# Another order for the 1290 steps of one kernel, other engines for a third of its small steps, and 19 fillers on TensorE where there were 48

## The chip, the cores and the metric

The kernel runs on one core of a Trainium2 chip. The metric is device time in microseconds (us). TensorE (PE in the profile) multiplies, VectorE (DVE), ScalarE (ACT) and GpSimd (POOL) do the elementwise work, and SyncE (SP) starts the transfers. Each engine carries out its own instructions strictly in the order in which the program gives them; engines wait for each other only where data or a buffer is concerned.

## The reference

Three stages follow each other, in float32:

```
attention (mLSTM), batch 2, 8 heads, 768 steps, head size 40, for every step t:
    m_new = max(f + m, i);  C = exp(f + m - m_new) * C + exp(i - m_new) * outer(v, k);  n likewise with k
    y[t] = sigmoid(o) * (C @ q) / max(|n . q|, 1)
x = y as 1536 tokens x 320
first layer:  xn = x / rms(x) * rms_g;  x1 = (silu(xn @ w_gate) * (xn @ w_val)) @ w_out     320 -> 1536 -> 320
second layer: h = x1 @ w_in;  out = (h * clip(h + 3, 0, 6) / 6) @ w_out                      320 -> 2048 -> 320
```

Every token of the second layer needs all of the first layer for that token, and the first layer needs the attention of that token; later chunks of the attention need the state of the earlier ones.

## The kernel before, in words

**Tiling.** The 768 positions are cut into 6 chunks of 128; a chunk c of a batch b is 128 tokens. The tokens form three groups of 512 (`G1`: chunks 0 and 1, 2 and 3, 4 and 5). In the first layer, group 0 is done for its first six column blocks in two parts of 256 tokens (`m0.0.0`: group 0, block 0, part 0), so that work can begin when only chunk 0 is ready; all else is done 512 tokens at a time.

**Exactness by two halves.** A matrix product takes float32 operands as two rounded parts: a value is rounded to `float32r` (the high part), and the difference is a second operand (the low part). So each activation is cast (`rounded`, L107) and subtracted (`sub`, L86), and TensorE multiplies high by high, high by low and low by high.

**Weights.** Weights come as 64-bit floats and are converted on the chip. `load_w` (L148, step `W`) loads one block of 640 KB, `conv` (L157, step `c`) turns its bits into float32 in several steps: low bits (L166 on ACT or L169 on DVE), sign (L173 or L176), scale (L180 or L183), joining (L186, always DVE), cast to the high part (L195 or L207), and the low part by `sub` (DVE or POOL). There are 34 blocks; 0 to 17 belong to the first layer, 18 to 33 to the second. Blocks 0 to 3 are loaded into the large pool, the others into two buffers (`rw`), so that a load from block 6 on waits for an earlier conversion to end.

**The order.** The program is cut into steps by `yield`. `PLAN` (L721) is a list of words, and each word carries out the next step of one task: `s` scores, `d` decay, `w` weighing, `a` product with v, `i` product with the state, `u` state update, `l` and `v` scaling of k and v, `n`, `D`, `e` the end of the attention, `x` the transposition into `xT` (a copy of the remaining columns `rem`, three transpositions into `ps_x`, the cast by ACT at L534, the subtraction by DVE at L536), `m` and `M` gate and val of the first layer, `o` its output product, `E` its evacuation, `X` the transposition for the second layer, `h` its hidden product (L628), its Relu (L632), product (L634), cast and `sub`, `p` its output product, `F` the results. The loop at L792 adds edges so that the instructions of each engine, the transfers of SyncE among them, stand in the order of the list (`issue_after`); such an edge is no wait on another engine.

**Fillers.** The word `H1` (`warm_up`, L706) runs two products of the identity into a PSUM tile that nobody reads; in the trace they are four instructions. There are 48 such words, all of them before the first step of the first layer.

**Engines.** `ENGINES` names for each weight block the engines of its six steps of free choice, `ON_DVE` the steps that run on DVE, and `REM` the engine of each `rem` copy. A step of `either` (L103) that isn't named in `ON_DVE` runs on POOL. The cast of an activation (`rounded`, words `K` in the first layer and `y` in the second) runs on ACT where it isn't named; in the kernel before none is named.

**Buffers around it.** The cast activations `g` have three buffers (`gp`): a cast waits until the output product that used the buffer has ended. PSUM has two tiles for `mm`, two for `ms` and four for the outputs `po`.

Of the kernel before, what the change touches and what calls it, by code (L numbers as in the profile page):

```python
# [7 lines left out]
F32 = mybir.dt.float32  # L8
# [10 lines left out]
def kernel(  # L19
# [15 lines left out]
    NC, B = qk.shape[:2]  # L35
# [54 lines left out]
    AADAPP AADADD AAAADP AADDPD AAAADP ADAADD DAAADD AADADP DAAADD AADADD DDAADP DAAAPP DDDDPD  # L90
    ADDADD ADDDDP DADADD DADADP ADADPD DAADPP AADADD ADAAPD AAAADD ADAAPP AADDPD DADADP AADADD
    DDAAPP DDDADD AAADDP ADDDPD ADAADP DDAADD DDADPP ADAADD
    """.split()
    ON_DVE = set("""
    v0.0 l0.1 e0.0 e0.1 v1.1 u1.0 u1.1 e1.0 e1.1 M0.0.1 M0.1.1 M0.2.0 M0.2.1 M0.4.1 M0.5.0
    M0.5.1 M0.6 M0.7 M0.8 M0.9 M0.11 E0.1 E0.2 v2.0 v2.1 u2.1 v3.0 v3.1 l3.1 u3.0 u3.1 e3.0 M1.1
    M1.3 M1.6 M1.10 E1.1 E1.2 l4.1 u4.1 l5.0 M2.1 M2.2 M2.4 M2.6 M2.9 M2.11 E2.0 E2.2 E2.3 h0.0
    h0.1 h0.2 h0.3 h0.5 h0.6 h0.7 h0.11 h0.13 h0.14 h0.15 h1.0 h1.1 h1.4 h1.8 h1.10 h1.11 h1.13
    h1.14 h1.15 h2.2 h2.3 h2.5 h2.6 h2.9 h2.15
    """.split())  # L100
    REM = "APDAADDDAAPPDDPPPADDPPPP"
# [265 lines left out]
    def decay(c, b):  # L367
        if c == b == 0:
            fbc[0] = ap2.tile([128, B, H, LS], F32, tag="fbc", name="fbc")
# [218 lines left out]

    def in1(gr, m, part=None):
        ts = tokens(gr, part)  # L590
        xT, N = xts[gr][:, :, :, ts], ts.stop - ts.start
        if N == 512:
            pg = pmm.tile([128, N], F32, tag="mm", name="gate")
        else:
            gv[gr, m, part] = pmm.tile([128, 2, N], F32, tag="mm", name="gv")
            pg = gv[gr, m, part][:, 0]
# [7 lines left out]
    def in1_val(gr, m, part=None):  # L604
        ts = tokens(gr, part)
        xT, N = xts[gr][:, :, :, ts], ts.stop - ts.start
        if N == 512:
            pool, tag = (pms, "ms") if gr == NG - 1 else (pmm, "mm")
            pv = pool.tile([128, N], F32, tag=tag, name="val")
        else:  # L610
            pv = gv[gr, m, part][:, 1]
# [110 lines left out]
    G0 L0 L1 W0 R k0.0 G1 k0.1 k1.0 q0.0 q0.1 W1 W2 W3 W4 W5 q1.0 C q1.1 C H1 C G0 H1 G0 H1 G0 G0 G1  # L722
    G0 H1 H1 c0 G0 G1 B0 c0 t0.0 G0 G1 G1 g0 B1 g0 t0.1 d0.0 g0 v0.1 G1 t1.0 v0.0 g0 H1 l0.0 g0 d0.1
    l0.0 H1 H1 H1 c0 l0.1 H1 l0.1 c0 u0 G1 c0 G1 G1 s0 c0 u0 H1 c1 w0.1 u0 g1 c1 H1 w0.0 c0 H1 c2 u0
    i0 c2 c1 c1 g1 H1 c2 q2.0 q2.1 H1 i0 c0 i0 c1 H1 c2 a0 c1 c4 c1 c2 c1 g1 c5 c5 g1 H1 n0.0 v1.0
    H1 c5 n0.1 H1 e0.0 g1 c2 H1 D0 H1 c4 c5 H1 c4 s1 e0.0 e0.1 c5 b1 b1 b2 b2 c4 H1 e0.0 H1 c5 c5
    k1.1 H1 c4 e0.1 H1 c4 c2 H1 e0.1 c4 H1 c3 k2.0 s2 c5 c3 e0.1 H1 e0.0 H1 e0.1 H1 e0.0 H1 d1.0
    x0.0 x0.0 H1 x0.0 d1.1 H1 l1.0 H1 H1 d2.0 l1.1 H1 H1 t1.1 H1 d2.1 H1 H1 t2.0 H1 w1.0 l1.0 H1
    w1.1 H1 l1.1 l2.0 H1 x0.0 x0.1 l2.1 c4 w2.1 x0.1 H1 x0.1 w2.0 H1 c2 W6 W7 x0.1 H1 m0.0.0 v1.1 c3
    v2.0 M0.0.0 m0.0.0 c3 u1 l2.0 M0.0.0 M0.0.0 u1 m0.1.0 c6 c6 u1 M0.0.0 c6 u1 M0.1.0 c3 c7 c6  # L730
    m0.2.0 m0.1.0 u1 c3 c7 M0.1.0 i1 m0.2.0 c6 c7 M0.2.0 q3.0 i1 q3.1 M0.1.0 i1 M0.1.0 a1 c7 M0.2.0
    c7 c6 c7 c7 o0.0.0 M0.2.0 W8 b3 b3 M0.2.0 n1.0 c7 m0.3.0 n1.1 D1 W9 M0.3.0 m0.3.0 e1.0 e1.1
    m0.4.0 e1.0 e1.1 e1.0 M0.4.0 c8 e1.1 k2.1 M0.3.0 e1.0 m0.4.0 k3.0 c8 m0.5.0 e1.1 M0.4.0 M0.3.0
    e1.0 c8 M0.5.0 e1.1 x1.0 m0.5.0 c8 x1.1 x1.0 x1.1 x1.0 d3.0 o0.1.0 x1.1 c9 o0.2.0 M0.5.0 M0.3.0
    l3.0 M0.4.0 x1.0 l2.1 t2.1 o0.3.0 x1.1 c8 M0.4.0 c8 m0.0.1 c8 t3.0 M0.5.0 v2.1 M0.0.1 c9 M0.5.0
    v3.0 m0.0.1 u2 c8 M0.0.1 l3.0 W10 M0.0.1 m0.1.1 c9 M0.0.1 c9 o0.0.1 m0.1.1 d3.1 c9 M0.1.1 c9
# [131 lines left out]
```

## Time and profile before

| what | value |
|---|---|
| median of 3 runs | 466.23 us (465.4 to 468.4) |
| the profiled execution | 462.94 us, its span 461.2 us |
| PE busy | 446.3 us, 97% of the span, 3936 matmuls |
| PE weight loads busy | 401.7 us, 87% |
| DVE, ACT, POOL busy | 252.7 us, 211.3 us, 127.7 us (55%, 46%, 28%) |
| fillers on PE (L710) | 192 instructions, 29.1 us |
| output products (L569) | 1008 instructions, 156.0 us |
| transfers | 37.06 MB by SyncE's queue; a weight block is 640 KB, a `kvo` 484 KB, half a `rawqk` 160 KB |

The shares are means over stages with different limits. A product's record also covers time in which the array works on its neighbours, so a busy PE says that something was in it, not that it ran at its best rate. The mean duration of a DVE instruction overlaps a little with the next, so that count times mean is more than the busy time.

### The profile page before, as it was taken

The numbers are of one execution on the slowest core, as the hardware profiler recorded it, in microseconds if no ns is written. First come the engines' busy times: TensorE is split into PE (matmuls) and PEld (weight loads), VectorE is DVE, ScalarE is ACT, GpSimd is POOL, SyncE is SP. The second block draws the span as 40 slices with busy tenths as digits, with TensorE's granted clock in tenths as the row PEclk, the third lists the DMA queues.
The fourth block names the chain that finished last, engine by engine and source line by source line (L and its number), as shares of the span: only waits on it lengthen the run. The fifth ranks groups of instructions, "written<-read, shape, count | busy, mean of one in ns | idle before, by whom it ended". The sixth has DMA issues, their size and how long they took to land.

```text
span 461.2 us, 9361 instructions
## 1 busy us (share of the span) xinstructions
PE 446.3 (97%) x3936; PEld 401.7 (87%) x3936; DVE 252.7 (55%) x442; ACT 211.3 (46%) x405; POOL 127.7 (28%) x151
## 2 busy tenths in 40 slices
PE   7999989989989999999999999999999999999996
PEld 6999979967878889898889899998989998899896
DVE  6688879889976433432455668862243214142321
ACT  5684665536462313222565565863433425152342
POOL 4405431433340322231324242231301321021241
PEclk9789989999998999999999999999999999999999
DMA  7974173484470000000323331230000100020002
GB/s 252 333 221 160 59 248 115 151 195 133 132 230 1 29 17 1 2 1 0 115 99 130 112 116 43 73 114 2 0 1 11 48 1 1 0 58 0 1 0 58
DMA packets 10906, 37.66 MB, mean 82 GB/s; under 512 B 1648, under 2 KB 3344, under 8 KB 10864
## 3 DMA queue, kind: packets, MB, share of 16 engines
q1 hardware_dynamic: 10864, 37.06, 24.5%
q8 instruction: 31, 0.51, 0.5%
q14 instruction: 11, 0.09, 0.1%
HBM read 35.05 MB, written 2.01 MB: 80 GB/s over the span
## 4 chain that ended last, share of the span: by engine, by line
PE 84%; DVE 6%; DMA 4%; ACT 2%; issue 1%; POOL 1%; SPq 0%; POOLq 0%; DVEq 0%; ACTq 0%
PE po L569 30%; PE hh L562 19%; PE gate L562 10%; PE val L562 10%; PE idle L710 5%; PE gv L562 4%; DMA fbc<-fsd 2%; PE ps_x L530 2%; DMA raw<-in_w_out_dram 2%; PE sc L281 1%; DMA raw<-in_w_gv_dram 1%; PE inter L281 1%; PE att L281 1%; PE U L281 1%; DVE e L615 1%
## 5 line engine op out<-in xcount | busy, mean ns | idle before, releaser
L569 PE MATMUL po<-w_out,g 128*128 128x320 f32 x1008 | 156.0, 311 | 0.0
L569 PEld LDWEIGHTS po<-w_out,g 128*128 128x128 f32 x1008 | 149.8, 189 | 1.9 <-DVE g L87 0.2
L562 PE MATMUL hh<-xT,w_in 128*128 128x512 f32 x384 | 89.8, 390 | 0.0
L562 PEld LDWEIGHTS hh<-xT,w_in 128*128 128x128 f32 x384 | 71.5, 188 | 14.2
L562 PE MATMUL gate<-xT,w_in 128*128 128x512 f32 x240 | 61.3, 402 | 2.1 <-ACT xT L534 1.3
L634 DVE SCALAR_TENSOR_TENSOR r<-r,hh 128x512 f32<-128x512 f32 x48 | 33.0, 687 | 50.6 <-ACT r L632 50.5
L562 PE MATMUL val<-xT,w_in 128*128 128x512 f32 x240 | 59.0, 392 | 0.0
L108 ACT CAST g<-r 128x512 fp32r<-128x512 f32 x48 | 29.8, 620 | 62.5 <-PE po L569 55.6
L87 POOL TENSOR_TENSOR g<-r,g 128x512 fp32r<-128x512 f32 x22 | 28.5, 1298 | 105.4 <-ACT g L108 101.7
L562 PEld LDWEIGHTS gate<-xT,w_in 128*128 128x128 f32 x240 | 45.4, 192 | 12.5 <-ACT xT L534 1.6
L562 PEld LDWEIGHTS val<-xT,w_in 128*128 128x128 f32 x240 | 44.5, 188 | 9.2
L632 ACT ACTIVATE r<-hh,three 128x512 f32<-128x512 f32 x48 | 33.0, 687 | 30.0 <-PE hh L562 19.5
L87 POOL TENSOR_TENSOR w_in<-raw,w_in 64x128 fp32r<-64x128 f32 (+1 forms) x37 | 29.2, 789 | 56.7 <-ACT w_in L195 23.0
L87 DVE TENSOR_TENSOR g<-r,g 128x512 fp32r<-128x512 f32 x26 | 18.3, 702 | 47.2 <-ACT g L108 47.2
L108 ACT CAST g<-e 128x512 fp32r<-128x512 f32 (+1 forms) x42 | 23.4, 557 | 41.9 <-DVE e L615 22.1
L615 DVE TENSOR_TENSOR e<-e,val 128x512 f32<-128x512 f32 x30 | 20.5, 683 | 34.1 <-PE val L562 33.2
L87 POOL TENSOR_TENSOR g<-e,g 128x512 fp32r<-128x512 f32 (+1 forms) x20 | 23.7, 1184 | 55.5 <-ACT g L108 41.9
L186 DVE SCALAR_TENSOR_TENSOR raw<-raw,bits 128x640 int32<-128x640 int32 x34 | 29.4, 869 | 5.5 <-ACT raw L180 5.3
L710 PE MATMUL idle<-ident 128*128 128x128 f32 x192 | 29.1, 317 | 1.6 <-POOL ident L119 1.6
L600 ACT ACTIVATE e<-gate 128x512 f32<-128x512 f32 x30 | 17.9, 595 | 25.5 <-PE gate L562 22.4
L710 PEld LDWEIGHTS idle<-ident 128*128 128x128 f32 x192 | 27.3, 228 | 2.0 <-POOL ident L119 1.5
L562 PE MATMUL gv<-xT,w_in 128*128 128x256 f32 x192 | 26.0, 289 | 2.1 <-DVE e L615 2.1
(114 smaller groups left out, 465.6 us busy)
## 6 DMA issues: line engine op xcount, KB each, us to landing
raw<-in_w_out_dram SPq DMA_DIRECT2D x14, 640.0 KB
raw<-in_w_gv_dram SPq DMA_DIRECT2D x12, 640.0 KB
kvo<-in_kvo_dram SPq DMA_DIRECT2D x12, 484.0 KB
raw<-in_w_in_dram SPq DMA_DIRECT2D x8, 640.0 KB
rawqk<-in_qk_dram SPq DMA_DIRECT2D x24, 160.0 KB
fbc<-fsd SPq DMA_DIRECT2D x10, 256.0 KB
out_dram<-o SPq DMA_DIRECT2D x6, 160.0 KB
out_dram<-o SPq DMA_DIRECT2D x12, 80.0 KB
```

The lines of the kernel that those rows point to most:

```text
L87: eng.tensor_tensor(out=out, in0=a, in1=hi.bitcast(F32), op=ALU.subtract)
L108: (nc.vector.tensor_copy if word in ON_DVE else nc.scalar.copy)(out=out, in_=in_)
L186: nc.vector.scalar_tensor_tensor(out=x, in0=hw, scalar=3, in1=y, op0=ALU.logical_shift_left, op1=ALU.bitwise_or)
L281: nc.tensor.matmul(start=True, stop=True, **kw)
L530: nc.tensor.transpose(out=ps[:, kk], in_=s, identity=ident)
L562: nc.tensor.matmul(out=ps, lhsT=w[:, wk], rhs=xT[:, hl, kk], start=(n == 0), stop=(n == len(seq) - 1))
L569: nc.tensor.matmul(out=ps, lhsT=g[:, gh, ts], rhs=w[:, wh, k % 2], start=(first and n == 0), stop=(last and n == 2))
L600: nc.scalar.activation(out=e, in_=pg, func=ACTF.Silu)
L615: nc.vector.tensor_tensor(out=e, in0=e, in1=pv, op=ALU.mult)
L632: nc.scalar.activation(out=r, in_=ps, func=ACTF.Relu, bias=three)
L634: nc.vector.scalar_tensor_tensor(out=r, in0=r, scalar=6.0, in1=ps, op0=ALU.min, op1=ALU.mult)
L710: nc.tensor.matmul(out=idle[i][:, 0:128], lhsT=ident, rhs=ident, start=True, stop=True)
```

## The change

The list is written in another order, with the same steps apart from the fillers (1290 words in all after it, 19 of them `H1`). Conversions of late blocks, the loads, the attention and the layers are interleaved otherwise; in the first layer a `val` may come before its `gate`, and chunk 0's decay may start with batch 1, for which `gate_and_val` and `decay` now take whichever comes first. `ENGINES`, `ON_DVE` and `REM` name other engines; 27 casts `y` and 15 casts `K` run on DVE. No instruction's shape changes.

```diff
@@ -87,18 +87,21 @@
         eng.tensor_tensor(out=out, in0=a, in1=hi.bitcast(F32), op=ALU.subtract)
 
     ENGINES = """
-    AADAPP AADADD AAAADP AADDPD AAAADP ADAADD DAAADD AADADP DAAADD AADADD DDAADP DAAAPP DDDDPD
-    ADDADD ADDDDP DADADD DADADP ADADPD DAADPP AADADD ADAAPD AAAADD ADAAPP AADDPD DADADP AADADD
-    DDAAPP DDDADD AAADDP ADDDPD ADAADP DDAADD DDADPP ADAADD
+    ADAAPP AAAADP AAAADP AAAADD AAADDD AAADPP AAADDD AAAAPP ADADDD AAAADD AADAPD AAAADP ADAADD
+    DAADPD DAAADP AAAADD ADAAPP AAAAPD DADAPP DADAPD AADADP ADDAPD DDDDPD ADDDDD DDADDP DDAADD
+    DDAADP DDDAPD ADAAPP ADAAPD ADADDD DDDADD DADAPP AAAADD
     """.split()
     ON_DVE = set("""
-    v0.0 l0.1 e0.0 e0.1 v1.1 u1.0 u1.1 e1.0 e1.1 M0.0.1 M0.1.1 M0.2.0 M0.2.1 M0.4.1 M0.5.0
-    M0.5.1 M0.6 M0.7 M0.8 M0.9 M0.11 E0.1 E0.2 v2.0 v2.1 u2.1 v3.0 v3.1 l3.1 u3.0 u3.1 e3.0 M1.1
-    M1.3 M1.6 M1.10 E1.1 E1.2 l4.1 u4.1 l5.0 M2.1 M2.2 M2.4 M2.6 M2.9 M2.11 E2.0 E2.2 E2.3 h0.0
-    h0.1 h0.2 h0.3 h0.5 h0.6 h0.7 h0.11 h0.13 h0.14 h0.15 h1.0 h1.1 h1.4 h1.8 h1.10 h1.11 h1.13
-    h1.14 h1.15 h2.2 h2.3 h2.5 h2.6 h2.9 h2.15
+    v0.1 l0.0 l0.1 u0.1 v1.0 e0.0 e0.1 l1.0 v1.1 l2.0 M0.0.0 u1.1 M0.1.0 e1.1 l2.1 M0.4.0 M0.5.0
+    l3.0 M0.0.1 M0.1.1 u2.1 M0.2.1 K0.5.1 e2.1 l3.1 M0.6 M0.7 u3.0 u3.1 M0.9 e3.0 e3.1 K0.11 v4.1
+    l4.1 M0.11 l5.0 u4.1 E0.2 K1.0 K1.1 e4.1 M1.2 l5.1 M1.3 e5.1 K1.7 M1.7 M1.9 K1.10 K1.11 K2.0
+    E1.0 E1.3 K2.1 M2.1 M2.2 M2.3 K2.4 K2.5 M2.5 M2.6 K2.7 K2.8 M2.8 K2.9 M2.9 K2.10 E2.0 E2.1 E2.3
+    y0.0 y0.3 h0.3 y0.4 h0.4 y0.5 y0.6 h0.6 y0.7 y0.8 y0.9 h0.9 h0.10 h0.11 h0.12 y0.14 h0.14 y0.15
+    h0.15 h1.0 y1.1 h1.1 y1.2 h1.2 y1.3 h1.3 y1.4 h1.4 y1.5 h1.5 y1.6 h1.7 h1.8 y1.9 h1.9 y1.10
+    h1.10 h1.11 h1.12 y1.15 y2.0 h2.0 y2.2 h2.2 y2.3 h2.3 h2.5 y2.7 h2.7 y2.10 y2.11 h2.12 h2.13
+    y2.14 h2.14 y2.15 h2.15
     """.split())
-    REM = "APDAADDDAAPPDDPPPADDPPPP"
+    REM = "AAAPPAAPDPDADDDADAPPDPDA"
 
     def either(step, *at):
         word = step + ".".join(str(i) for i in at if i is not None)
@@ -365,8 +368,8 @@
         yield
 
     def decay(c, b):
-        if c == b == 0:
-            fbc[0] = ap2.tile([128, B, H, LS], F32, tag="fbc", name="fbc")
+        if c == 0 and c not in fbc:
+            fbc[c] = ap2.tile([128, B, H, LS], F32, tag="fbc", name="fbc")
         d = fbc[c][:, b].rearrange("p h t -> p (h t)")
         src = fps[b].rearrange("p h t -> p (h t)") if c == 0 else d
         nc.vector.tensor_tensor_scan(out=d, data0=src, data1=inject.rearrange("p h t -> p (h t)"),
@@ -586,14 +589,18 @@
     def tokens(gr, part):
         return slice(0, 256 * len(G1[gr])) if part is None else slice(256 * part, 256 * part + 256)
 
+    def gate_and_val(gr, m, part, N):
+        if (gr, m, part) not in gv:
+            gv[gr, m, part] = pmm.tile([128, 2, N], F32, tag="mm", name="gv")
+        return gv[gr, m, part]
+
     def in1(gr, m, part=None):
         ts = tokens(gr, part)
         xT, N = xts[gr][:, :, :, ts], ts.stop - ts.start
         if N == 512:
             pg = pmm.tile([128, N], F32, tag="mm", name="gate")
         else:
-            gv[gr, m, part] = pmm.tile([128, 2, N], F32, tag="mm", name="gv")
-            pg = gv[gr, m, part][:, 0]
+            pg = gate_and_val(gr, m, part, N)[:, 0]
         mm_in(pg, wi1[m], 0, xT)
         yield
         e = ep.tile([128, 512], F32, tag="e", name="e")[:, 0:N]
@@ -608,7 +615,7 @@
             pool, tag = (pms, "ms") if gr == NG - 1 else (pmm, "mm")
             pv = pool.tile([128, N], F32, tag=tag, name="val")
         else:
-            pv = gv[gr, m, part][:, 1]
+            pv = gate_and_val(gr, m, part, N)[:, 1]
         mm_in(pv, wi1[m], 1, xT)
         yield
         e = gs[gr, m, part]
@@ -719,71 +726,70 @@
-    G0 L0 L1 W0 R k0.0 G1 k0.1 k1.0 q0.0 q0.1 W1 W2 W3 W4 W5 q1.0 C q1.1 C H1 C G0 H1 G0 H1 G0 G0 G1
-    G0 H1 H1 c0 G0 G1 B0 c0 t0.0 G0 G1 G1 g0 B1 g0 t0.1 d0.0 g0 v0.1 G1 t1.0 v0.0 g0 H1 l0.0 g0 d0.1
-    l0.0 H1 H1 H1 c0 l0.1 H1 l0.1 c0 u0 G1 c0 G1 G1 s0 c0 u0 H1 c1 w0.1 u0 g1 c1 H1 w0.0 c0 H1 c2 u0
-    i0 c2 c1 c1 g1 H1 c2 q2.0 q2.1 H1 i0 c0 i0 c1 H1 c2 a0 c1 c4 c1 c2 c1 g1 c5 c5 g1 H1 n0.0 v1.0
-    H1 c5 n0.1 H1 e0.0 g1 c2 H1 D0 H1 c4 c5 H1 c4 s1 e0.0 e0.1 c5 b1 b1 b2 b2 c4 H1 e0.0 H1 c5 c5
-    k1.1 H1 c4 e0.1 H1 c4 c2 H1 e0.1 c4 H1 c3 k2.0 s2 c5 c3 e0.1 H1 e0.0 H1 e0.1 H1 e0.0 H1 d1.0
-    x0.0 x0.0 H1 x0.0 d1.1 H1 l1.0 H1 H1 d2.0 l1.1 H1 H1 t1.1 H1 d2.1 H1 H1 t2.0 H1 w1.0 l1.0 H1
-    w1.1 H1 l1.1 l2.0 H1 x0.0 x0.1 l2.1 c4 w2.1 x0.1 H1 x0.1 w2.0 H1 c2 W6 W7 x0.1 H1 m0.0.0 v1.1 c3
-    v2.0 M0.0.0 m0.0.0 c3 u1 l2.0 M0.0.0 M0.0.0 u1 m0.1.0 c6 c6 u1 M0.0.0 c6 u1 M0.1.0 c3 c7 c6
...
-    i3 c17 c16 m0.10 c17 M0.10 c16 q5.0 c16 q5.1 i3 c17 i3 a3 M0.10 c16 M0.10 W18 W19 M0.10 m0.11
-    n3.0 b5 b5 n3.1 e3.0 e3.1 D3 M0.11 m0.11 e3.0 e3.1 e3.0 k4.1 c18 c18 o0.8 M0.11 e3.0 e3.1 e3.0
-    c19 k5.0 e3.1 c19 o0.9 x3.0 e3.1 c18 x3.1 c19 M0.11 c19 x3.0 x3.1 c18 x3.0 o0.10 x3.1 x3.0 v4.1
-    t4.1 x3.1 l4.1 t5.0 m1.0 d5.0 M0.11 l5.0 m1.1 m1.0 d5.1 l5.0 l5.1 u4 v5.0 m1.1 u4 o0.11 u4 u4 u4
...
-    p2.9 h2.11 h2.13 h2.11 h2.13 p2.10 h2.12 h2.14 h2.12 h2.14 p2.11 h2.13 h2.15 h2.13 h2.15 p2.12
-    h2.14 h2.14 p2.13 h2.15 h2.15 z0 F2 F2 z1 F2 F2 z2 F2 F2 z3 F2 F2
+    G1 L0 G0 G0 G0 W5 G0 G0 G0 c5 C H1 L1 c5 W4 W1 C c5 c4 G0 H1 G1 G1 H1 c4 c4 c5 H1 c4 G1 G1 c1 B1
+    k0.1 G0 C c4 c4 G1 W0 g0 g0 g0 k0.0 W2 q0.1 c5 B0 c0 G1 c4 c0 d0.1 d0.0 q0.0 l0.1 c0 c4 H1 l0.0
+    l0.0 c0 G1 l0.1 b1 c1 c1 b1 g0 W3 c2 c2 v0.1 c1 W6 H1 v0.0 u0 G1 q1.1 u0 g0 H1 u0 c5 u0 c5 t0.0
+    H1 s0 i0 H1 H1 H1 H1 w0.0 d1.0 t0.1 c1 i0 c0 i0 w0.1 c2 q1.0 c0 c6 c5 c2 d1.1 c0 c6 c6 a0 c3 c2
+    H1 l1.1 W7 g1 c3 c2 R n0.0 s1 n0.1 e0.0 D0 g1 g1 e0.0 k1.0 e0.1 e0.1 g1 c6 c0 e0.1 e0.0 H1 l1.0
+    H1 c7 c6 e0.1 w1.0 e0.1 q2.0 c6 l1.0 c3 b2 c7 H1 H1 v1.0 g1 e0.0 k1.1 t1.1 W9 e0.0 H1 l1.1 x0.0
+    H1 b2 x0.1 c3 x0.0 x0.0 x0.1 v1.1 u1 w1.1 x0.0 x0.1 x0.1 M0.0.0 c2 q2.1 c7 c1 u1 u1 u1 c2 c1
+    M0.2.0 c7 m0.0.0 c3 m0.2.0 c1 u1 m0.0.0 i1 M0.0.0 m0.1.0 t1.0 d2.0 k2.1 c9 c3 i1 m0.2.0 c7 i1 c9
+    c7 M0.1.0 M0.2.0 d2.1 l2.1 a1 n1.1 q3.0 n1.0 m0.4.0 M0.0.0 M0.0.0 M0.4.0 e1.1 m0.1.0 s2 D1
...
+    m0.10 M0.9 n3.1 t4.0 x2.0 n3.0 c15 D3 x2.0 x2.0 c16 x2.1 e3.1 M0.10 m0.10 c16 e3.0 e3.0 x2.0 c16
+    e3.0 M0.8 c15 c15 M0.11 M0.10 e3.0 e3.1 e3.1 c15 M0.8 o0.7 e3.1 e3.1 M0.9 m0.11 o0.8 m0.11 e3.0
+    x3.1 l4.0 x2.1 b5 x3.0 M0.9 x3.1 x2.1 x3.1 k4.1 l4.1 x3.0 o0.9 M0.10 x3.0 x3.1 t4.1 x3.0 k5.0
+    m1.2 m1.2 M0.11 v4.1 u4 m1.1 M0.11 M0.11 m1.4 W17 b5 u4 u4 u4 d5.1 c17 c17 u4 c17 m1.1 M1.1
...
+    h2.13 h2.13 p2.9 h2.13 h2.10 h2.15 h2.15 h2.14 p2.10 h2.12 h2.12 h2.13 h2.12 p2.11 h2.12 p2.12
+    p2.13 h2.14 h2.15 h2.14 h2.14 h2.15 h2.14 z0 F2 z1 F2 F2 F2 z2 z3 F2 F2 F2 F2
```

## Rows read from the trace of the kernel before

**Rows 1.** Windows: start, middle and rest; per engine busy us (instructions), clock, DMA share, GB/s.

```profile
0.00:45.60 45.60, 42.19 (x686) 40.23 (x686) 34.96 (x66) 27.41 (x59) 17.05 (x37) 0.89 0.72 242
45.60:137.90 92.30, 85.24 (x1147) 76.44 (x1145) 80.27 (x156) 51.61 (x111) 32.11 (x36) 0.98 0.51 159
137.90:461.20 323.30, 318.92 (x2107) 285.03 (x2107) 137.43 (x223) 132.26 (x236) 78.55 (x79) 0.99 0.11 37
```

**Rows 2.** Timeline of PE near 40 us: start, us, line, operation, idle before.

```profile
38.22 5.97 PE L710 MATMUL idle<-ident 128*128 128x128 f32 x52
44.02 0.38 PE L530 MATMUL ps_x<-ident,y 128*128 128x128 f32 x2
45.67 2.17 PE L562 MATMUL gv<-xT,w_in 128*128 128x256 f32 x16
```

**Rows 3.** Timeline of DVE in the same place.

```profile
34.87 1.07 DVE L515 SCALAR_TENSOR_TENSOR y<-y,ss,gbc 128x320 f32<-128x320 f32 x2 [0.16 <-POOL ss L513]
35.86 5.05 DVE L372 TENSOR_TENSOR_SCAN fbc<-fbc,inject 128x512 f32<-128x512 f32 x4
45.06 0.56 DVE L536 TENSOR_TENSOR xT<-ps_x,xT 128x384 fp32r<-128x384 f32 x1 [1.31 <-ACT xT L534]
```

**Rows 4.** Timelines of ACT, DVE and PE before the first product of group 1.

```profile
133.05 0.93 ACT L166 ACTIVATE bits<-raw 128x640 uint16<-128x640 uint16 x1 [1.31 <-DMA raw<-in_w_out_dram]
...
134.78 0.50 DVE L183 TENSOR_SCALAR raw<-raw 128x640 f32<-128x640 f32 x1 [1.57 <-ACT bits L173]
...
137.86 5.30 PE L562 MATMUL gate<-xT,w_in 128*128 128x512 f32 x15 [0.66 <-DVE xT L536]
```

**Rows 5.** Groups by form, DVE conversion steps: busy us, mean ns of one, idle before.

```profile
L186 DVE SCALAR_TENSOR_TENSOR raw<-raw,bits 128x640 int32<-128x640 int32 x34 | 29.4, 869 | 5.5 <-ACT raw L180 5.3
L183 DVE TENSOR_SCALAR raw<-raw 128x640 f32<-128x640 f32 x16 | 10.0, 622 | 4.3 <-ACT bits L173 3.7 <-issue 0.4 <-DVE g L87 0.2
L87 DVE TENSOR_TENSOR w_in<-raw,w_in 128x512 fp32r<-128x512 f32 x13 | 9.6, 748 | 2.3 <-ACT w_in L195 2.3
L176 DVE TENSOR_SCALAR bits<-raw 128x640 uint16<-128x640 uint16 x15 | 8.9, 593 | 1.7 <-DMA raw<-in_w_in_dram 0.9 <-DMA raw<-in_w_out_dram 0.6 <-DMA raw<-in_w_gv_dram 0.2
L87 DVE TENSOR_TENSOR w_out<-raw,w_out 128x640 fp32r<-128x640 f32 x9 | 8.1, 900 | 3.2 <-ACT w_out L207 3.1
L169 DVE TENSOR_SCALAR bits<-raw 128x640 uint16<-128x640 uint16 x13 | 8.1, 620 | 6.1 <-DMA raw<-in_w_in_dram 4.5 <-DMA raw<-in_w_gv_dram 0.9 <-DMA raw<-in_w_out_dram 0.6
```

**Rows 6.** Waits of PE over the whole span: us in total, times, longest.

```profile
PE gv L562 <- DVE e L615: 2.1, 1, 2.1
PE sc L281 <- DMA rawqk<-in_qk_dram: 1.6, 2, 1.2
```

**Rows 7.** Pieces of the chain of waits, for PE's rate: start, us, what.

```profile
28.14 2.88 PE idle L710 x24
...
159.71 1.09 PE sc L281 x64
...
439.22 17.61 PE po L569 x120
```

**Rows 8.** Waits of ACT's casts, and of PE's weight loads for the casts' outcome.

```profile
ACT g L108 <- PE po L569: 75.3, 39, 8.3
...
PEld po L569 <- ACT g L108: 0.2, 1, 0.2
```

**Rows 9.** Groups by form: casts on ACT, and one of the same width on DVE.

```profile
L108 ACT CAST g<-r 128x512 fp32r<-128x512 f32 x48 | 29.8, 620 | 62.5 <-PE po L569 55.6 <-DVE r L634 6.8
L195 DVE CAST w_in<-raw 128x512 fp32r<-128x512 f32 x4 | 1.7, 422 | 0.0
```

**Rows 10.** Windows within two stretches of half clock (columns as in the first group).

```profile
23.10:26.10 3.00, 3.00 (x46) 2.92 (x39) 2.07 (x4) 1.79 (x4) 0.06 (x1) 0.50 0.67 235
64.00:67.10 3.10, 3.10 (x16) 3.10 (x15) 3.06 (x6) 1.56 (x5) 0.00 (x0) 0.50 0.97 386
```

**Rows 11.** Page, transfer rate in the 40 slices of 11.5 us.

```profile
GB/s 252 333 221 160 59 248 115 151 195 133 132 230 1 29 17 1 2 1 0 115 99 130 112 116 43 73 114 2 0 1 11 48 1 1 0 58 0 1 0 58
```

## What I predicted before the result was known

> **What bounds the kernel now.** The page alone says "TensorE, 97%", and that misleads, because the fillers and slow stretches count as busy. So I first cut the span in the windows where the order changes character [rows 1]: up to the first product of the first layer (45.6 us), from there to the first product of group 1 (137.9 us), and the rest. In the rest, PE is busy for 318.9 of 323.3 us, and most of the difference is the tail after the last product: nothing but less TensorE work or a better clock helps there. In the middle PE is busy for 85.2 of 92.3 us, DVE for 80.3: two engines, each nearly full, that stop each other. In the start much of PE's time is fillers.
>
> The timelines at the two joins then show what ends each stage. At the first, the last two tokens' `y` is ready at 35.94, yet the second transposition begins at 44.0, behind 52 filler instructions, and DVE meanwhile does four decays, 5.05 us; the last `xT` ends at 45.6 [rows 2, 3]. At the second, ACT takes up a step of weight block 19 whose data came late, and DVE waits 1.57 us for a conversion step, both in front of the `xT` that the `gate` product at 137.86 needs [rows 4]. Block 19 belongs to the second layer, which is more than 100 us away. The middle is lost to conversions done too early.
>
> **The change, part by part.** *Start.* I counted the words up to the first product and multiplied each kind by its mean duration. DVE has 39.4 us of work before and 38.3 after; before, 35.0 us of busy time [rows 1] answer to it, a factor of 0.88 for overlapping records, used on every DVE sum below. What differs is the place. Before the last `y`, DVE has 31.8 us in the old list and 35.0 in the new, so the last `y` comes 2.8 us later (3.2 x 0.88), at 38.7. Between it and the last `xT`, where the old list has the decays and takes 9.7 us, the new one has one joining step, a scaled v, one weighing and the two subtractions, 3.3 us, so 2.9; I add 0.9 for the hand-overs between DVE, ACT and PE that so little work doesn't hide. First product at 42.5 instead of 45.7: **-3.2 us**. Both `rem` copies are on ACT now instead of ACT and POOL.
>
> *Fillers.* 29 words fewer are 116 instructions, 13.9 us at 2.88 us for 24 [rows 7]. I price that at nothing of its own: PE's real work before the first product is only 13.5 us, and what the fillers cost is already in the 42.5.
>
> *Middle.* Up to the first product of group 1 the old list has 18 conversions finished and two begun, the new one 17. On DVE that is, by [rows 5]: joining 20 to 17 (-2.6), scale 11 to 1 (-6.2), low bits 8 to 2 (-3.7), sign 6 to 4 (-1.2), `w_in` subtraction 10 to 6 (-3.0), `w_out` subtraction 3 to 5 (+1.8). The other kinds (casts, scaled v and k, `rem`, one product of the first layer) add up to -0.6. Together -15.5 us over both stages, of which the middle has -14.4: 91.5 down to 77.1, so 67.7 us of busy time where there were 80.3. ACT takes some of it (+5.4 us up to this point, on 79.0 busy of 137.9 us [rows 1]) and is covered by its idle time. POOL's work up to there falls by 3.2 us.
>
> With DVE relieved, PE becomes the limit: its 85.2 us less one output product that the new list puts later (12 instructions, 1.76 us [rows 7]) are 83.5. Of the 7.1 us of PE's idle time I keep 1.6, the wait of `sc` for a load, which isn't the conversions' doing [rows 6], and 0.7 for new hand-overs: 85.8 instead of 92.2, **-6.4 us**. The bounds are 79.7 (DVE's 67.7 plus its present 12.0 idle) and 92.2.
>
> *Rest.* The output product comes back, **+1.8 us**. Conversions of blocks 17 to 19 and 42 of the 90 casts move to DVE there: 174 instead of 143 us of DVE work, in 325 us, where DVE is now busy for 137 [rows 1]. A cast costs 0.62 us on ACT; the nearest row on DVE, of the same width, is 0.42 [rows 9]. The idle time of DVE hides them, and if that cover goes, PE's next output product waits (third rival). The loads are reordered on SyncE's queue: ahead of the first `kvo` now stand three weight blocks and the gates (2.1 MB instead of 0.9), and ahead of the last `rawqk` of chunk 0 5.0 MB instead of 3.1. At 333 GB/s [rows 11] the latter is 15 us. Ahead of the first weighing, which needs those scores, the new list has 20.0 us of DVE work (17.6 busy), so the loads are hidden; uncovered they would cost up to the 5.7 us that the 1.9 MB more take. Bounds 0 and +5.7, and I take 0, nearer to the cover; the loads of later blocks wait for a free buffer as now. The new handling of `gv` and of chunk 0's decay adds no instruction. The four words at the very end change places on engines that don't wait for each other: 0.
>
> Sum: -3.2 - 6.4 + 1.8 = -7.8. The profiled execution goes from 462.9 to 455.1; it lies 3.3 below the median, so the median goes from 466.2 to **458.4**.
>
> **The rivals.** *Deeper.* If the hand-overs are filled at both joins, the first product stands near DVE's own limit (33.7 us busy and half of the 10.6 idle that it has now in the 45.6, so 39) and the middle takes 82 (PE's 83.5 without its stretch of half clock, 1.6): 39 + 82 against 42.5 + 85.8, 7.3 us more gained, and a cleaner rest 1.6: 449.5. For it: the new list starts almost nothing early that isn't needed. Against: both engines would be above 80% without disturbing each other.
>
> *Fillers were needed.* The clock is at half, 1.2 GHz, in both windows of [rows 10]: at 64 us, a little after PE had waited 2.1 us for DVE [rows 6], and at 23 us, behind a stretch of small products, with PE busy all the time. So work of some kind doesn't by itself hold the clock, which speaks against the fillers' worth, but an idle gap was followed by half clock. Without 29 of them the start has more gaps. If five blocks on the attention's path (scores, state, weighed v, update, transposition; 1.09 us for 64 instructions [rows 7]) run at half clock, that is 5.4 us; three more half-clock stretches like that at 64 (3.1 us, half of it lost) are 4.7. Together +10.1: 468.5, no change that can be measured. The Trainium skill, TensorE: Matmul & The Clock Gate, section "Why this matters for your kernels", says to keep TensorE busy without gaps, since activity is what lifts the half clock; by that rule alone the fillers earned their place and this rival is the forecast. The trace agrees at 64 us and not at 23.
>
> *Slower: casts block DVE.* ACT's casts wait 75.3 us in all for an output product to release a buffer [rows 8]. If 42 of 90 casts take their share of these waits to DVE, 35.1 us, everything behind them on DVE waits too, first of all the products at L615 and L634 that release PE's PSUM tiles. If half of it reaches PE, +17.6: 476.0. The case is slower by over 1% from 12.5 us of PE time on, 0.30 us per cast. Against it: the same waits now stand on ACT before the Relu and Silu steps, which PE needs just as much, and PE's weight loads waited only 0.2 us for ACT's casts [rows 8]. For it: the new list lets fewer casts come right behind the release, but also uses the two `mm` tiles more tightly.
>
> **How the numbers follow.** A measurement tells from no change what differs by about 1%, 4.7 us. Chances: forecast 0.45, with its own range 451 to 464 (start -5 to 0 and middle 82 to 89); deeper 0.15; fillers needed 0.22; casts block DVE 0.13; 0.05 for late loads and the like, near no change. Below 461.6 lie most of the forecast, the deeper case and a little of the second rival: 0.60 faster. Above 470.9 lie the third rival and a tail of the second: 0.15. The rest, 0.25, is the same. The range 446 to 470 leaves out the third rival and the lower end of the deeper case, some 0.18.
>
> **What would show it.** Right: first `gv` product at 40 to 44 us with few fillers before it; first 512-column `gate` at 125 to 131; no conversion step of block 17 or later in front of `xT` there; DVE near 80% in the middle and near 50% after; PE without gaps in the rest. Wrong: PE waiting for DVE's `e`, `r` or `g` in the rest (third rival), half clock through the start or after it (second), or a first product no earlier than now because `y` waits for its loads.

## The result, and the profile after

The changed kernel takes 450.1 us (median of 4 runs, 448.9 to 451.8) where the kernel before takes 465.8 (4 runs, 460.7 to 468.4): a ratio of 0.970, 95% interval 0.961 to 0.979. That is 15.7 us less by the medians. The profiled execution went from 462.9 to 449.4, 13.5 less, and its span from 461.2 to 447.7; the explanation is made against these 13.5. I had forecast 7.8 less, 458.4, with a range from 446 to 470: right in its sign and inside the range, at half the size. (Ratios here and below use undisturbed executions alone, so they can differ a little from a quotient of medians, and the profiled execution of experiment 4 was a disturbed one, of which only the place of a wait is read.)

First two rows of the page of the kernel after: busy time by engine, and the chain that ended last (the profile's own chain of work, followed back from the last instruction), by engine.

```profile
PE 433.6 (97%) x3820; PEld 389.4 (87%) x3820; DVE 265.4 (59%) x471; ACT 199.5 (45%) x389; POOL 118.6 (27%) x138
...
PE 94%; DMA 3%; DVE 1%; SPq 1%; ACT 0%; issue 0%; ACTq 0%
```

PE is "97%" as before, and this says as little as before. The last row says more: from the start of the work to its end, the chain now hardly leaves TensorE (94%, where the page before had 84%). Then the same three windows as in [rows 1] (up to the first `gv` product, up to the first `gate` product of group 1, the rest):

```profile
0.00:43.20 43.20, 34.41 (x571) 31.55 (x571) 33.24 (x65) 30.27 (x60) 14.08 (x32) 0.96 0.76 253
43.20:123.40 80.20, 79.20 (x1136) 72.19 (x1131) 69.75 (x132) 52.23 (x116) 32.32 (x42) 1.00 0.49 161
123.40:447.70 324.30, 319.95 (x2122) 285.63 (x2120) 162.40 (x276) 117.00 (x214) 72.24 (x66) 1.00 0.13 43
```

| stage | before | after | difference | forecast |
|---|---|---|---|---|
| start | 45.6 | 43.2 | -2.4 | -3.2 |
| middle | 92.3 | 80.2 | -12.1 | -6.4 |
| rest | 323.3 | 324.3 | +1.0 | +1.8 |
| span | 461.2 | 447.7 | -13.5 | -7.8 |

So nine tenths of the gain come from the middle. The PE timeline after, around the two joins [rows 2, 4]:

```profile
35.37 1.16 PE L284 MATMUL sc<-rawqk 40*64 40x64 f32 x64
...
36.84 4.57 PE L717 MATMUL idle<-ident 128*128 128x128 f32 x24
...
42.12 1.14 PE L284 MATMUL U<-kvo 64*64 64x41 f32 x64
43.20 4.26 PE L565 MATMUL gv<-xT,w_in 128*128 128x256 f32 x32
...
121.58 2.00 PE L572 MATMUL po<-w_out,g 128*128 128x320 f32 x12
123.42 2.02 PE L565 MATMUL gate<-xT,w_in 128*128 128x512 f32 x8
```

Before, the second join had a lone `gate` instruction at 136.71, a gap, and the run of them at 137.86; now an output product leads into eight `gate` instructions with no gap. At the first join 32 `gv` instructions follow each other. The DVE timeline at the first join [rows 3]:

```profile
39.75 0.54 DVE L518 SCALAR_TENSOR_TENSOR y<-y,ss,gbc 128x320 f32<-128x320 f32 x1
40.21 0.82 DVE L189 SCALAR_TENSOR_TENSOR raw<-raw,bits 128x640 int32<-128x640 int32 x1
40.95 0.49 DVE L385 TENSOR_TENSOR kvo<-kvo,gT 128x328 f32<-128x328 f32 x1
41.36 0.68 DVE L420 TENSOR_TENSOR fbc<-sc,fbc 128x512 f32<-128x512 f32 x1
42.42 1.02 DVE L539 TENSOR_TENSOR xT<-ps_x,xT 128x384 fp32r<-128x384 f32 x2 [0.38 <-ACT xT L537]
```

Between the last `y` and the last `xT` stand exactly the joining, the scaled v, the weighing and the two subtractions that I had counted, and no decay. PE's waits over the whole span (columns: total us, times, longest) are few:

```profile
PE ps_g L292 <- DVE ga L268: 6.0, 1, 6.0
PE idle L717 <- POOL ident L122: 1.5, 1, 1.5
...
PE gv L565 <- ACT e L607: 0.5, 1, 0.5
PE gv L565 <- DVE e L622: 0.5, 1, 0.5
```

The first two lie in the start. After the first `gv` product only the last two stand, 1.0 us; of [rows 6], the wait for DVE's `e` went from 2.1 to 0.5 us and that for `rawqk` is gone, and so are those for `xT` at the second join [rows 4].

### The profile page after: what moved, and what is told of

The parts are those of the page before. It is cut to its first block, busy times and chain, and to the rows that moved or that the text cites. A ratio compares the mean times of both kernels' runs of the same rounds, so it can differ in the third digit from the quotient of the medians.

```text
span 447.7 us, 9139 instructions
## 1 busy us (share of the span) xinstructions
PE 433.6 (97%) x3820; PEld 389.4 (87%) x3820; DVE 265.4 (59%) x471; ACT 199.5 (45%) x389; POOL 118.6 (27%) x138
## 4 chain that ended last, share of the span: by engine, by line
PE 94%; DMA 3%; DVE 1%; SPq 1%; ACT 0%; issue 0%; ACTq 0%
PE po L572 33%; PE hh L565 20%; PE gate L565 13%; PE val L565 12%; PE gv L565 5%; PE idle L717 2%; DMA rawqk<-in_qk_dram 2%; PE ps_x L533 2%; PE sc L284 2%; DMA raw<-in_w_gv_dram 2%; PE att L284 2%; PE U L284 1%; PE inter L284 1%; SPq L114 1%; PE ps_g L292 0%
## 5 line engine op out<-in xcount | busy, mean ns | idle before, releaser
L572 PE MATMUL po<-w_out,g 128*128 128x320 f32 x1008 | 157.8, 310 | 0.0
L565 PE MATMUL hh<-xT,w_in 128*128 128x512 f32 x384 | 93.0, 392 | 0.0
L565 PE MATMUL gate<-xT,w_in 128*128 128x512 f32 x240 | 59.7, 394 | 0.0
L87 POOL TENSOR_TENSOR g<-r,g 128x512 fp32r<-128x512 f32 x18 | 24.5, 1369 | 106.6 <-DVE g L111 52.3
L87 POOL TENSOR_TENSOR w_in<-raw,w_in 64x128 fp32r<-64x128 f32 (+1 forms) x38 | 31.2, 822 | 74.1 <-ACT w_in L198 35.4
L169 ACT ACTIVATE bits<-raw 128x640 uint16<-128x640 uint16 x23 | 21.5, 933 | 11.7 <-DMA raw<-in_w_out_dram 6.9
L87 DVE TENSOR_TENSOR g<-r,g 128x512 fp32r<-128x512 f32 x30 | 21.4, 721 | 8.2 <-ACT g L111 7.9
L565 PEld LDWEIGHTS gv<-xT,w_in 128*128 128x128 f32 x192 | 23.8, 191 | 1.7 <-ACT e L607 0.7
L111 ACT CAST g<-r 128x512 fp32r<-128x512 f32 x21 | 12.9, 618 | 26.9 <-PE po L572 25.4
```

The costliest lines, as they stand in the source:

```text
L87: eng.tensor_tensor(out=out, in0=a, in1=hi.bitcast(F32), op=ALU.subtract)
L111: (nc.vector.tensor_copy if word in ON_DVE else nc.scalar.copy)(out=out, in_=in_)
L169: nc.scalar.activation(out=u[:, :, 0], in_=ru[:, :, 1], func=ACTF.Copy, scale=2.0 ** -13, bias=-0.49997)
L565: nc.tensor.matmul(out=ps, lhsT=w[:, wk], rhs=xT[:, hl, kk], start=(n == 0), stop=(n == len(seq) - 1))
L572: nc.tensor.matmul(out=ps, lhsT=g[:, gh, ts], rhs=w[:, wh, k % 2], start=(first and n == 0), stop=(last and n == 2))
```

## The experiments

In the table, "middle" ends at the first `gate` instruction of group 1 and "rest" at the last PE instruction, so that for the kernel before they are 91.0 and 320.1. Ratios are to the kernel before, run on the same chip.

| kernel | start | middle | rest | median, us | ratio, 95% interval |
|---|---|---|---|---|---|
| before | 45.7 | 91.0 | 320.1 | 464 to 466 | |
| after | 43.2 | 80.2 | 319.9 | 450.1 | 0.970 (0.961 to 0.979) |
| 1 order only | 46.8 | 94.5 | 324.4 | 471.6 | 1.021 (1.017 to 1.026) |
| 2 engines only | 47.3 | 98.6 | 318.2 | 471.7 | 1.023 (1.017 to 1.029) |
| 3 fewer fillers, before | 43.4 | 93.1 | 321.7 | 466.0 | 1.008 (1.005 to 1.011) |
| 4 blocks 18, 19 later, before | not read | | | 464.3 | 0.999 (0.996 to 1.003) |
| 5 old conversion engines | 48.8 | 88.5 | 325.2 | 468.4 | 1.013 (1.007 to 1.019) |
| 6 old step engines | 48.4 | 83.7 | 323.4 | 460.3 | 0.995 (0.991 to 1.000) |
| 7 casts on ACT | 43.3 | 80.2 | 319.9 | 451.1 | 0.976 (0.970 to 0.983) |
| 8 no fillers | 45.0 | 81.5 | 319.9 | 453.1 | 0.981 (0.975 to 0.986) |
| 9 gates first | 44.9 | 80.2 | 319.9 | 451.3 | 0.970 (0.962 to 0.978) |
| 10 gates first, fillers there | 43.9 | 80.2 | 319.9 | 450.7 | 0.969 (0.960 to 0.977) |
| 11 scores early | 43.2 | 80.2 | 319.9 | 449.6 | 0.968 (0.957 to 0.979) |
| 12 gate transfer early | 43.9 | 80.2 | 319.9 | 449.6 | 0.965 (0.957 to 0.974) |

**1. The order alone.** The changed kernel with the three engine settings of the kernel before:

```diff
     ENGINES = """
-    ADAAPP AAAADP AAAADP AAAADD AAADDD ...
+    AADAPP AADADD AAAADP AADDPD AAAADP ...
     ON_DVE = set("""
-    v0.1 l0.0 l0.1 u0.1 v1.0 e0.0 ...
+    v0.0 l0.1 e0.0 e0.1 v1.1 u1.0 ...
-    REM = "AAAPPAAPDPDADDDADAPPDPDA"
+    REM = "APDAADDDAAPPDDPPPADDPPPP"
```

> The new list of steps (19 fillers) with the engines of the kernel before (ENGINES, ON_DVE and REM as they were). Theory A, DVE's work ahead of group 1 sets the middle: with the old engines the new list still has 125.3 us of DVE work there (131.0 before, 115.5 after), so a third of the relief: about -5 in the middle and -2.5 in the start, 455 to 459 us where the kernel before has 465. Theory B, the place of the steps in front of xT is what counts and the engines hardly matter: 450 to 452, like the changed kernel. Theory C, the engines are the gain and the order is worth nothing: 463 to 466.

**2. The engines alone.** The kernel before with the three settings of the changed one:

```diff
     ENGINES = """
-    AADAPP AADADD AAAADP AADDPD AAAADP ...
+    ADAAPP AAAADP AAAADP AAAADD AAADDD ...
...
-    REM = "APDAADDDAAPPDDPPPADDPPPP"
+    REM = "AAAPPAAPDPDADDDADAPPDPDA"
```

> The old list of steps (48 fillers) with the new engines. Theory A: DVE's work ahead of the first product of group 1 falls from 131.0 to 122.3 us, 7.6 us of busy time, so 457 to 460 us. Theory B (place only): 463 to 466, the xT of group 1 still stands behind blocks 18 and 19. Theory C (engines are the gain): 450 to 453. If the casts moved to DVE block PE in the rest of the kernel, PE gaps appear after 138 us and the time is above 466.

Both came out slower than before, by 2.1% and 2.3%, and the whole change is 3.0% faster. None of the theories A to C gave either time. The last theory of the second text gave a time above 466, but not for its reason: the rest is no longer than before (318.2 against 320.1 us). The windows of the middle, of the first and of the second:

```profile
46.81:141.28 94.47, 85.41 (x1136) 75.38 (x1131) 80.73 (x151) 43.05 (x103) 30.75 (x36) 0.96 0.45 141
```

```profile
47.34:145.94 98.60, 87.87 (x1142) 77.99 (x1143) 76.38 (x138) 59.28 (x123) 31.09 (x38) 0.96 0.49 153
```

The second falsifies the simple form of my reason. DVE has less to do than before (76.4 us against the 79.0 that it has in the kernel before up to 136.71), and yet the middle is 7.6 us longer. DVE's sum of work doesn't set it; what stands where in the queues does. The end of the chain of waits of the second kernel (start, us, what) shows which work it is:

```profile
132.99 0.47 POOL w_in L87
...
133.48 8.06 DMA raw<-in_w_out_dram
...
141.56 0.92 ACT bits L176
142.49 0.15 ACT rem L527
...
142.68 0.78 PE ps_x L533 x4
```

A weight block was loaded when a conversion released its buffer, took 8.06 us, and the conversion step that waited for it stood in ACT's queue in front of the small `rem` copy that PE's transposition needs. In the kernel before, the same load ends the middle by way of DVE:

```profile
125.78 7.18 DMA raw<-in_w_out_dram
...
133.85 0.91 ACT bits L173
...
134.78 0.51 DVE raw L183
...
137.26 0.56 DVE xT L536
...
137.86 2.36 PE gate L562 x7
```

In the middle of the kernel before, the chain has 19.7 us in transfers in all (a `w_gv` load, a decay's broadcast `fbc`, this one), 22.7 on DVE, 9.3 on ACT and 30.4 on PE. In the changed kernel it has no transfer in the middle at all, 77.2 us on PE, 1.3 on ACT and 1.1 on DVE. For the order alone the chain in the profile, followed back from the end, breaks off at 179 us, so that for that kernel the waits in the middle could not be followed back; of PE's own waits there the longest are for DVE's state (`st`, 3.9 us in all) and for `e` of ACT (2.0).

**3. Fewer fillers, in the kernel before.** The last 29 of its 48 `H1` words left out:

```diff
-    H1 c5 n0.1 H1 e0.0 g1 c2 H1 D0 H1 c4 c5 H1 c4 s1 ...
+    H1 c5 n0.1 H1 e0.0 g1 c2 D0 c4 c5 c4 s1 ...
```

> The kernel before with its last 29 fillers taken out, among them the 52 instructions in front of the second transposition; all else as before. Mine: worth nothing or a little, 463 to 466 us, because DVE's decays still stand in front of the xT; the first product moves by at most the 1.3 us that DVE waited there. Rival, the fillers held the clock: several us slower, 468 to 472, with half clock from the start into the first layer. Rival, the fillers themselves were the loss: -5 or more, below 461.

The kernel isn't faster: 1.008, interval 1.005 to 1.011. Its PE timeline at the first join:

```profile
28.66 2.14 PE L281 MATMUL sc<-rawqk 40*64 40x64 f32 x128
...
36.31 0.66 PE L530 MATMUL ps_x<-ident,y 128*128 128x128 f32 x2 [5.52 <-DVE y L515]
...
41.74 0.47 PE L530 MATMUL ps_x<-ident,rem 128*128 128x128 f32 x1 [4.13 <-POOL rem L524]
43.39 0.55 PE L562 MATMUL gv<-xT,w_in 128*128 128x256 f32 x1 [1.17 <-DVE xT L536]
44.96 1.44 PE L562 MATMUL gv<-xT,w_in 128*128 128x256 f32 x5 [1.02 <-DVE xT L536]
```

The first transposition begins 5.5 us after the work in front of it, and then the `rem` copy on POOL and the decays in front of `xT` stop it instead. One lone product goes 2.3 us earlier, the run of them 0.7 us earlier than [rows 2], and the middle still ends at 136.46. What the fillers had hidden was a wait, not room. The pace falls in that wait, too. The 128 score products in front of it take 2.14 us, 1.07 for 64; behind it two transpositions take 0.66 us where they took 0.38 [rows 2], and the granted clock stays at half into the first layer:

```profile
36.00:47.00 11.00, 4.37 (x16) 3.44 (x17) 10.86 (x15) 4.08 (x10) 6.36 (x8) 0.50 0.43 158
```

How much of the 0.8% comes from this pace is not separated; the rest is 1.6 us longer, too (321.7 against 320.1), for a reason that I did not find.

**4. Two late blocks moved behind group 1's first product, in the kernel before.** The words `W18 W19`, four `c18` and four `c19`:

```diff
-    ... c16 M0.10 W18 W19 M0.10 m0.11 ...
+    ... c16 M0.10 M0.10 m0.11 ...
...
-    t4.1 x3.1 l4.1 t5.0 m1.0 d5.0 M0.11 ...
+    t4.1 x3.1 l4.1 t5.0 m1.0 W18 W19 c18 c18 c19 c19 c18 c19 c19 c18 d5.0 M0.11 ...
```

> The kernel before with the ten steps of weight blocks 18 and 19 (two loads, eight conversion steps) moved from in front of the first product of group 1 to right behind it. Theory A: 3.0 us less DVE work there, 2.6 us of busy time, 462 to 463 us. Theory B, the late data of block 19 hold up ACT and DVE in front of xT: the wait of 1.3 on ACT, 1.6 on DVE and the 4 us of steps behind it go, so -4 to -6, 459 to 461, and PE's gap before the first gate product of group 1 is gone. Rival: nothing, since the two loads then come late and the stall moves to the conversions of group 1's blocks.

No change: 0.999. Of its PE timeline, the wait that follows the second join:

```profile
144.75 0.85 PE L569 MATMUL po<-w_out,g 128*128 128x320 f32 x4 [2.21 <-DVE g L87]
```

The join itself has no gap any more, and one of 2.2 us stands some 8 us behind it, where a product waits for a `g` that DVE gives out late. The chain shows why:

```profile
132.49 6.63 DMA raw<-in_w_out_dram
...
139.94 0.93 ACT bits L173
...
144.11 0.59 DVE g L87
```

It is a late load again, with its conversion steps on ACT and DVE, which now stand in front of `g` instead of `xT`. Moving the words that the profile blames doesn't help: the wait goes where they go.

**5 and 6. The engines, by halves.** The changed kernel with the old `ENGINES` alone (the conversions), and with the old `ON_DVE` and `REM` alone (all other steps). The edits are the two parts of the diff of experiment 1:

```diff
     ENGINES = """
-    ADAAPP AAAADP AAAADP AAAADD AAADDD ...
+    AADAPP AADADD AAAADP AADDPD AAAADP ...
```

```diff
     ON_DVE = set("""
-    v0.1 l0.0 l0.1 u0.1 v1.0 e0.0 ...
+    v0.0 l0.1 e0.0 e0.1 v1.1 u1.0 ...
-    REM = "AAAPPAAPDPDADDDADAPPDPDA"
+    REM = "APDAADDDAAPPDDPPPADDPPPP"
```

> The changed kernel with the weight conversions on the engines of the kernel before (ENGINES alone goes back). DVE's work ahead of group 1 rises from 115.5 to 125.2 us, ACT's falls from 90.9 to 79.3. Theory A2, in the new list it is DVE's conversion work that limits the middle: most of the loss of the run with all old engines (471.6) is here, 462 to 472 us, middle at 90 or more. Theory D, a list fits its engines and any set put back costs in proportion: about half, 458 to 462. Rival, conversions don't matter: 449 to 453.

> The changed kernel with the other steps on the engines of the kernel before (ON_DVE and REM go back, so also no cast on DVE; ENGINES stays new). DVE's work ahead of group 1 is 115.6 us, as in the changed kernel; scaled k and v, states and low parts move between DVE and POOL. Theory A2: 450 to 454 us, the middle stays near 80. Theory D, steps in the wrong queue cost by what waits for them, POOL being half as fast: 458 to 464, with waits of TensorE for scaled k, states or low parts.

The old conversion engines cost 18.3 us of the changed kernel's 450.1, the old step engines 10.2, both together (experiment 1) 21.5. The windows of the middle, of the first and of the second:

```profile
48.76:137.30 88.54, 83.26 (x1135) 74.12 (x1131) 78.06 (x144) 42.35 (x102) 32.12 (x39) 0.98 0.42 136
```

```profile
48.38:132.07 83.69, 80.35 (x1137) 72.37 (x1131) 73.04 (x138) 52.09 (x116) 30.63 (x37) 1.00 0.49 156
```

With the old conversion engines DVE has 78.1 us in the middle where the changed kernel has 69.8, ACT 42.4 instead of 52.2, and all three stages are longer. So the conversions that went from DVE to ACT do carry the larger part. The chain in the middle of that kernel has 28.8 us on DVE (1.1 in the changed kernel) and 7.9 in two loads, so that there DVE's own steps are what ends it for the most part. But the list's DVE work ahead of group 1 (words by kind, times the mean of one) is 115.6 us with the old step engines and 115.5 in the changed kernel, and the middles are 83.7 and 80.2: the same sum, 3.5 us apart. By that same count the order alone has 125.3 and a middle of 94.5, the old conversion engines 125.2 and 88.5, the kernel before 131.0 and 91.0. The time of the old step engines is that of theory D, but not by the waits that it names: PE's longest waits behind the start are for ACT's `e` (1.6 us) and `g` (1.3).

**7. All casts back on ACT.** The 42 words `y` and `K` taken out of the changed kernel's `ON_DVE`:

```diff
-    l3.0 M0.0.1 M0.1.1 u2.1 M0.2.1 K0.5.1 e2.1 l3.1 M0.6 M0.7 u3.0 u3.1 M0.9 e3.0 e3.1 K0.11 v4.1
+    l3.0 M0.0.1 M0.1.1 u2.1 M0.2.1 e2.1 l3.1 M0.6 M0.7 u3.0 u3.1 M0.9 e3.0 e3.1 v4.1 ...
...
```

> The changed kernel with all 42 casts K and y back on ACT; the list and all other engines as changed. Only two of the casts stand before group 1, so the middle (80.2 us) stays. Mine: DVE had room for them and ACT has too (117 of 324 us busy in the rest), so the rest moves by under 1%: 449 to 454 us. Rival, the list puts these casts where DVE is early, and on ACT they queue behind the waits for buffers: gaps of PE in the rest, 455 us and more. Rival, casts on DVE blocked PE after all: faster, 447 or less.

The time is that of the changed kernel, 451.1 against 450.1, with overlapping intervals. Its rest:

```profile
123.56:443.49 319.93, 319.93 (x2122) 285.61 (x2120) 151.04 (x248) 132.36 (x240) 70.76 (x66) 1.00 0.13 42
```

DVE has 11.0 us less and ACT 15.7 us more to do than the changed kernel has in its rest up to the last PE instruction, and PE is busy without a break in both. So in this order it makes no measurable difference which of the two engines has the casts.

**8. No fillers.** The changed kernel without its 19 `H1` words:

```diff
-    ... c5 C H1 L1 c5 W4 W1 C c5 c4 G0 H1 G1 G1 H1 c4 ...
+    ... c5 C L1 c5 W4 W1 C c5 c4 G0 G1 G1 c4 ...
```

> The changed kernel without its 19 fillers. Mine: the start stays at 43 us or falls by up to 1, since the last 24 filler instructions end as the transposed data come ready; then the first products run at half clock, and as PE is the limit of the middle, each such stretch of 3 us costs 1.6: 450 to 453 us. Rival, fillers are worth nothing or less: 448 to 450. Rival, without them the clock stays low for long: over 456.

453.1 against 450.1; the intervals of the ratios overlap, but the profiles agree on 3.0 us (span 450.7 against 447.7). The window of its start, and PE's timeline there:

```profile
0.00:44.98 44.98, 22.98 (x495) 20.60 (x495) 34.52 (x66) 31.14 (x63) 16.36 (x33) 1.00 0.73 244
```

```profile
32.84 1.99 PE L284 MATMUL sc<-rawqk 40*64 40x64 f32 x64
...
41.66 0.66 PE L533 MATMUL ps_x<-ident,y 128*128 128x128 f32 x2 [6.20 <-DVE y L518]
...
43.10 1.95 PE L284 MATMUL U<-kvo 64*64 64x41 f32 x64
```

The transposition waits 6.2 us for `y`, and the 64 products of the state update behind it then take 1.95 us; in the changed kernel they take 1.14 in the same place. The wait is not what slows them: the 64 score products in front of it already take 1.99 us, as those at 21.80 do (1.97), where the changed kernel's at 35.37 take 1.16. So without fillers PE is at half pace in every piece of the start that I compared (the clock of 1.00 in the window is no evidence against it, see the last section), and with them it had come out of half pace by 35 us. By the chain, transpositions and state update take 1.5 us longer than in the changed kernel, of the 1.8 by which the start is longer; the first 32 `gv` products take 4.97 us instead of 4.26, 0.7 of the middle's 1.2. That pace is most of what the 19 fillers are worth.

**9 to 12. A shorter start.** With middle and rest at PE's own rate, only the start was left. 9: the second gates load `L1` goes right behind the first. 10: as 9, with four more fillers behind `B1`. 11: as 9, but the four fillers behind `B1` are those that stood before the weighing, and the scores `s0` come ahead of the state update. 12: as 11, and `B0` follows `B1`. The edit of 12, which holds the others':

```diff
-    G1 L0 G0 G0 G0 W5 G0 G0 G0 c5 C H1 L1 c5 W4 ... c1 B1
-    k0.1 ... q0.1 c5 B0 c0 G1 ... v0.0 u0 ... H1 s0 i0 H1 H1 H1 H1 w0.0
+    G1 L0 L1 G0 G0 G0 W5 G0 G0 G0 c5 C H1 c5 W4 ... c1 B1
+    B0 H1 H1 H1 H1 k0.1 ... q0.1 c5 c0 G1 ... v0.0 s0 u0 ... H1 i0 w0.0
```

> The changed kernel with the second load of the gates (80 KB) ahead of weight block 5 instead of behind it. In the changed kernel DVE waits 2.2 us for it. Theory S, the start is a sum of DVE's waits (3.1 and 2.2 us for gates, 2.0 for the scores, 1.5 for the weighed v): -1 to -2, first product at 41 to 42 us, 448 to 449. Rival, the start hangs on the loads of q and k that come behind all weight blocks: nothing, 450.

> As the run with the gates first, plus four fillers in the 6 us in which TensorE waits for the transposition of the gates. If the start runs at half clock for want of work (scores of 64 instructions took 1.92 us there, 1.09 in the kernel before), scores and state products get full clock: another -1, 447 to 448. If an early filler doesn't lift the clock until the scores, nothing more: as that run.

> The changed kernel with the gates first, four of its fillers moved from behind the first state product to that early gap of TensorE, and chunk 0's scores put ahead of its state update, so that they don't stand behind scaled v. Theory S: the waits of DVE for scores (2.0) and weighed v (1.5) shrink too, -3 to -4 in all: first product at 39 to 40.5, 446 to 447.5. Rival, the q loads land at 19 us and the update behind the scores now waits: no better than the gates first alone.

> As the run with the scores early, and the spreading of batch 0's decay factors put right behind that of batch 1, ahead of the transposition of the gates for which TensorE waits. DVE is busy at that time with conversions anyway, so mine: within 1 us of that run. Rival, the decays begin earlier and everything behind them: another -2.

None beats the changed kernel beyond what can be measured (451.3, 450.7, 449.6, 449.6), and no start is shorter than 43.2. The waits that I took away came back elsewhere. The four early fillers of 10 did not lift the pace for the scores: these still take 1.99 us there. In the kernel with early scores the weighing no longer waits for PE's `sc` (2.0 us in the changed kernel) but for ACT:

```profile
DVE fbc L420 <- ACT last L395: 2.9, 1, 2.9
```

My reason there, that the start is the sum of DVE's work and of its waits, so that each wait taken away shortens it, has fallen. In all four the last `y` is ready at 40.0 to 40.6 us, as in the changed kernel (40.3), and the transposition begins only at 41.4 to 42.9. What stands between them can be read from the chain that ended last. In 9, 10 and 11 it is the 24 fillers in front of the transposition, which take 4.5 to 5.4 us, against 2.88 at full clock [rows 7]; in 12 the chain goes over a load of `kvo`, whose step on ACT stands in front of the `rem` copies. First DVE's last `y` and the chain with the gates first, then the chain of 12:

```profile
40.06 0.55 DVE L518 SCALAR_TENSOR_TENSOR y<-y,ss,gbc 128x320 f32<-128x320 f32 x1
```

```profile
37.70 5.42 PE idle L717 x24
43.12 0.81 PE ps_x L533 x6
```

```profile
36.78 4.62 DMA kvo<-in_kvo_dram
...
41.48 0.47 ACT kvo L390
...
41.95 0.20 ACT rem L527
```

So the fillers that lift the pace also hold up the first transposition, by up to 2.3 us. Why `y` itself comes no earlier stays open, and no run leaves out the last 24 filler instructions alone.

What the four do show is the floor for these products: in the four, in the changed kernel and in that with the casts on ACT, six kernels with starts from 43.2 to 44.9, the middle is 80.2 and the rest 319.9, the same to 0.05 us.

## Why the prediction was right, point by point

**Start: right in size, 0.7 us too short.** First product at 43.2, forecast 42.5. The last `y` came at 40.3 instead of 38.7, 1.6 late. From there to the first product it took 2.9 where I had put 3.8, since one half of the products begins before the last `xT` ends, at 43.44. Two small errors against each other. My term was a sum of DVE's work; the chain that ended last runs on PE alone from 20.88 us to the first product, 10.6 us of it fillers, and its last 24 filler instructions end 1.0 us after `y`. DVE and PE came to the join at nearly the same time, so that the agreement is in part luck.

**Fillers: priced at nothing, and worth a little.** Leaving 29 out in the old order costs 0.8% (experiment 3); the 19 that stay are worth some 3 us (experiment 8). The rival in which fillers were needed was right in its mechanism, and its price was too high: in experiment 3 a wait of 5.5 us was followed by half pace up to 47 us, and in experiment 8 PE was still at half pace at the first join. Half clock through the start was also one of my signs of being wrong, and by the pace of the products it came, in the changed kernel as well (64 score products in 1.99 us at 23.91, last section); the start was still 2.4 us shorter than before, and what the pace cost there isn't separated. The rule of the Trainium skill (TensorE: Matmul & The Clock Gate, section "Why this matters for your kernels"), to keep TensorE busy, points the right way here. But of the 24 fillers at 36.84 most ran at 1.2 GHz (granted clock 0.57 from 37.0 to 40.5 us) although PE had not been idle since 31.9.

**Middle: the right mechanism, and the mis-sized term.** I wrote that DVE would fall to 67.7 us and that PE would become the limit. DVE has 69.8, and PE is the limit, with 1.0 us of idle time. But I took PE's 85.2 us less one output product, 83.5, for its work; in the changed kernel as many products (a state update of 64 went to the start, 64 score products came in for it) are 79.2 us busy. That is 4.3 of the 5.6 us by which the middle is shorter than forecast; the other 1.3 are idle time (1.0, forecast 2.3). Of the 4.3, about 1.7 are the clock: half of the time from 64 to 67.4 us, in which it was granted at half before [rows 10] and not after. Another 0.6 lies at the edges of the window before, which holds the lone `gate` instruction at 136.71 and the end of the fillers. The other 2.0 I couldn't separate. A busy share is no rate: PE's floor should have come from counts of products times the rate of an undisturbed row, as [rows 2] and [rows 7] allowed for all but `gate` and `val`. The lower bound that I had given, 79.7, came from DVE and met it by chance. Two signs came out otherwise than stated: the first `gate` at 123.4, before the 125 to 131 that I gave, and DVE busy for 87% of the middle, not near 80%.

The reason for the gain needs a correction too. I put it as a sum of DVE's work; experiments 2 and 6 show that the sum doesn't decide. What the chains of the kernel before, of the engines alone and of experiment 4 show is a late load of 6.6 to 8.1 us, with its conversion steps in front of `xT`, `rem` or `g` on an engine that works in order. The changed kernel has no such load on its chain in the middle. That this is the whole cause is read from the chains and not isolated: the one experiment that moved a late load (4) moved the wait along, and with the old conversion engines (5) it is mostly DVE's own steps that stand on the chain.

**Rest: right.** +1.0 where I had +1.8. DVE is at 50% there (162 of 324 us), as forecast, and PE waits for nothing.

**Rivals.** "Deeper" gave 449.5, nearest to 450.1 in the sum, yet by another split: a start of 39 and a middle of 82. The start never came below 43.2, the middle went below 82. "Casts block DVE" is refuted (experiment 7). The waits that I shared out shrank: ACT's 75.3 us [rows 8] are 31.7 on ACT and 9.8 on DVE in the changed kernel. With all casts on ACT in the new order they are 34.4 there, so that it isn't the engine of the casts that shortened them.

## What to carry to other kernels

On in-order engines, the list of steps and the choice of engines are one setting: here each half of the change made the kernel 2% slower and both together 3% faster, so half of such a change is no test of it. Where the chain that ends a stage runs through a late load, ask which step waiting for it stands in front of the work that PE needs; making the stage before shorter (experiment 3), or the sum of an engine's work smaller (experiment 2), gave nothing here. Take PE's floor from counts and the rate of an undisturbed stretch; once a stage runs there, only the other stages are worth a trial. Fillers lifted the pace of what followed here, and stood in its way: compare when they end with when the data behind them are ready.

## What the runs showed that I had not expected

The row of the granted clock can mislead in the start of a profile. From 20 to 25 us PE's busy time is the same to 0.01 us in the changed kernel and in the one with the gates first, with a granted clock of 1.00 in one and of 0.50 in the other. First the changed kernel:

```profile
20.00:25.00 5.00, 4.59 (x99) 4.14 (x98) 3.84 (x7) 4.69 (x12) 1.27 (x2) 1.00 0.92 281
```

```profile
20.00:25.00 5.00, 4.60 (x100) 4.15 (x99) 3.56 (x6) 4.70 (x11) 1.44 (x3) 0.50 0.90 273
```

The products agree with the lower level, 1.2 GHz: in the changed kernel (timeline of PE), where the row says 1.00, eight fillers take 2.07 us and 64 score products 1.99, and in the gates-first kernel, where it says 0.50, they take the same. At full clock 24 fillers took 2.88 us and 64 score products 1.09 [rows 7]. In the kernel without fillers the row says 1.00 throughout, and 64 score products take 1.99 us at 32.84.

```profile
23.91 1.99 PE L284 MATMUL sc<-rawqk 40*64 40x64 f32 x64
```

```profile
23.62 1.99 PE L284 MATMUL sc<-rawqk 40*64 40x64 f32 x64
```

In these profiles the row stands at 1.00 up to the first change that it records (37 us in the changed kernel), whatever the pace. So much of the start ran at half pace in both, and mean granted clocks of 0.996 and 0.97 over these two spans are no difference between the kernels.
